# Paired blocks from unit 8, loads held until a transpose is through, a new load order in the lead-in, and V of units 1 to 7 scaled by GpSimd

## The chip, the cores and the metric

The kernel runs on one core of a Trainium2 chip. The metric is device microseconds of that core, median over runs. Before the change it was 311.35 us (three runs, 311.02 to 311.6).

## The reference, cut to what matters

```python
q, k, v: (8 batches, 8 heads, 576 positions, 64)      # float32
scores = q @ k.T / 8;  D[i, j] = gamma_h ** (i - j) if i >= j else 0
attn   = (scores * D) @ v                              # retention, no softmax
x      = attn as (8*576, 512)
h      = x @ w_in;  out = (h * sigmoid(1.702 * h)) @ w_out   # 512 -> 2048 -> 512
```

The kernel cuts the 4608 rows into 36 *units* of 128 rows and keeps a running state k^T v per batch. Four units make a *chunk* of 512 rows for the MLP; `up` is one group of four 512-column matmuls with `w_in`, `down` one group of four with `w_out`. Decay factors go into V (`vfac`) and into the eviction of the result (`gq`).

Of the kernel before, what the change touches and what calls it, by code (L numbers as in the profile page):

```python
# [6 lines left out]
AF = mybir.ActivationFunctionType  # L7
# [6 lines left out]
P = 128  # L14
HP = H // 2
# [6 lines left out]
def gamma(h):  # L22
    return 1.0 - 2.0 ** (-5.0 - h)
# [117 lines left out]
def bass_retnet_parallel__then__act_gelu_quick_kernel(  # L141
# [13 lines left out]
    with es:  # L155
# [11 lines left out]
        iota_k = sb("iota_k", [P, 4], FP32)  # L167
        iota_t = sb("iota_t", [P, 1], FP32)
        scr = sb("scr", [P, 1], FP32)
# [40 lines left out]

        def load_v(u, eng="pool"):
            sl = u % NVN
            rows = unit_rows(u)

            def f(e):
                return [
                    e.dma_start(  # L217
                        vn[sl][p0 : p0 + n, :, :],
                        v[b, :, s0 : s0 + n, :].rearrange("h p d -> p h d"),
                    )  # L220
                    for p0, n, b, s0 in rows
                ]
            op(eng, f, writes=[f"vn{sl}"], dma=f"d_vn{sl}_{eng}", ndma=len(rows))

# [44 lines left out]

        def setup_last():  # L270
            for hp in range(HP):
                op("act", lambda e, hp=hp: e.activation(
                    gq[:, 4, hp, :].rearrange("p (t i) -> p t i", i=64),
                    iota_c[:, None, 512:576].to_broadcast([P, 2, 64]),
                    AF.Exp, bias=lnsc.ap(), scale=lng[:, hp : hp + 1]),
                   reads=["iota_c", "lnsc", f"lng{hp}_0", f"lng{hp}_1"], writes=[f"gq{hp}_4"])
            op("dve", lambda e: e.tensor_scalar_add(iota_t[0:64], iota_k[0:64, 0:1], 512.0),
               reads=["iota_k"], writes=["iota_t0"])
            op("dve", lambda e: e.tensor_scalar_add(iota_t[64:128], iota_k[64:128, 0:1], 448.0),
               reads=["iota_k"], writes=["iota_t1"])  # L280
            for h in range(H):
                op("act", lambda e, h=h: e.activation(
                    vfac[:, 4, h : h + 1], iota_t.ap(), AF.Exp, scale=-math.log(gamma(h))),
                   reads=["iota_t0", "iota_t1"], writes=[f"vfact{h}"])

# [4 lines left out]
        def setup_tail():  # L290
            op("dve", lambda e: e.tensor_single_scalar(maskc.ap(), dmat.ap(), 0.0, ALU.is_ge),
               reads=["dmat"], writes=["maskc"])
            op("dve", lambda e: e.memset(maskc[0:64, 64:128], 0.0), reads=["maskc"], writes=["maskc"])
            for j in range(4):
                op("dve", lambda e, j=j: e.memset(kv[1][j].ap(), 0.0), writes=[f"kv1_{j}"])

        VF = [f"vfac{h}" for h in range(H)]
        VFT = [f"vfact{h}" for h in range(H)]

        def scale_v(u):  # L300
            sl, _, ty = u % NVN, *unit_info(u)[1:]
            op("dve", lambda e: e.tensor_tensor(  # L302
                vp[u % NVP].ap(), vn[sl].ap(),
                vfac[:, ty, :, None].to_broadcast([P, H, DH]), ALU.mult),
               reads=[f"vn{sl}"] + (VF if ty < 4 else VFT), writes=[f"vp{u % NVP}"])
# [248 lines left out]
        def head_mid(u):  # L554
            scale_v(u)
            head_s(u)
# [4 lines left out]

        def fetch(m, after=()):
            for u in (2 * m, 2 * m + 1):
                if u < NU:
                    load_kq(u, after)
                    load_v(u)

# [9 lines left out]

        def block(m, done=False):

            a, b = 2 * m, 2 * m + 1  # L580
            nxt = 2 * m + 2 < NU
            if not done:
                inter(a)
                inter(b)
            if nxt:
                scores(a + 2)
                scores(b + 2)
                scores_out(a + 2, 0)
            if not done:
                values(a)  # L590
                values(b)
                values_out(a)
                values_out(b)
            if nxt:
                scores_out(a + 2, 1)
                scores_out(b + 2, 0)
                scores_out(b + 2, 1)
            fetch(m + 4)
            ready_t(m + 3)
            ready_v(m + 2)  # L600

# [18 lines left out]
        setup_gq(1, 4)  # L620
        setup_last()
        for u in range(1, 4):
            load_kq(u)
            load_v(u)
        for i in range(4):
            load_win(i)
        for u in range(4, 8):
            load_kq(u)
            load_v(u)
        for i in range(4):  # L630
            load_wout(i)
        for u in (8, 9):
            load_kq(u)
            load_v(u)

# [14 lines left out]
        scale_v(0)  # L650
        scale_v(1)
        transpose_half(1, 0, "S2", "act")
        warm(4)
        transpose_half(1, 1, "H0", "act")
        head_k(0, "act")
        head_v(0)
        head_s(1)
        scale_v(2)
        transpose_half(2, 0, "S2", "act")
        warm(2)  # L660
        transpose_half(2, 1, "H0", "act")
        head_k(1, "act")
        head_s(2)
        scale_v(3)
        head_v(1)
        transpose_half(3, 0, "S2", "act")
        transpose_half(3, 1, "H0", "act")
        head_k(2, "act")
        setup_gelu()
        head_s(3)  # L670
        head_v(2)
        warm(3)
        head_v(3)
        head_k(3, "act")
        setup_tail()
        for u in (10, 11):
            load_kq(u)
            load_v(u)
        warm(2)
        play(16, lambda f: up(0, f), {  # L680
# [6 lines left out]
        })  # L687
        fetch(6)
        head_mid(6)
        head_in(7, "dve")  # L690
        warm(1)
        play(8, lambda i: up_half(1, i, 0), {
            1: [lambda: head_out(6)],
# [3 lines left out]
        play(8, lambda i: up_half(1, i, 1), {  # L697
            2: [lambda: head_in(8, "dve")],
            4: [lambda: head_mid(8)],
            6: [lambda: head_out(8)],  # L700
            7: [lambda: head_in(9, "dve")],
        })
        ready_t(6)
        fetch(7, [f"qkT{13 % NQT}q"])
        play(16, lambda i: down(0, i, ("H0", "H1")), {
            1: [lambda: head_mid(9)],
            3: [lambda: head_in(10, "dve"), lambda: head_out(9)],
            5: [lambda: head_mid(10)],
            7: [lambda: head_in(11, "dve"), lambda: head_out(10), lambda: ready_t(7), lambda: fetch(8, [f"qkT{15 % NQT}q"])],
            9: [lambda: head_mid(11), lambda: ready_v(6)],  # L710
            11: [lambda: head_out(11)],
        })
        late = None
        for m in range(5, NU // 2 + 1):
            if m < NU // 2:
                block(m, m == 5)
            if late is not None:
                up(*late)
            c, h = divmod(m - 1, 2)
            iu = idn = 0  # L720
            for x in "UUDDUDUDUDUDDDUU" if m == 5 else "DDUDUDUDUDUDDUUU":
                if x == "D":
                    down(c - 1, 8 * h + idn, YB)
                    idn += 1
# [70 lines left out]
```

## The kernel before: the parts that the change and the argument touch

One helper records every operation and derives the semaphore waits from the tiles it reads and writes. Each engine executes its own list in order, also GpSimd and SyncE, which issue the DMAs.

```python
NLD, NVN, NQT, NVP = 12, 10, 10, 6          # buffers of k/q, V, transposed k/q, scaled V

def load_kq(u, after=()): ...                # two loads on the GpSimd queue, float32 -> bf16
def load_v(u, eng="pool"): ...               # one load on the GpSimd queue
def scale_v(u): op("dve", ... vp[u % NVP] = vn * vfac ...)          # VectorE
def transpose_pe(u, bank, eng): ...          # 8 TensorE transposes and one eviction
def transpose_dma(u):                        # the same by a DMA transpose, on the SP queue
    op("sp", lambda e: e.dma_start_transpose(qkT[u % NQT].ap(), ...), ...)

def scores(u, sb0=None): ...     # 8 matmuls on half the array's rows, banks S0,S1 or S2,S3
def scores_out(u, hh, ...): ...  # VectorE: mask product PSUM -> pm
def values(u, ...): ...          # 8 matmuls on half the array's columns, bank O0 or O1
def inter(u, ...): ...           # q times the running state, whole array
def down(c, i, ybanks): ...      # 4 matmuls; every 4th: ScalarE evicts to osb (4 buffers),
                                 # SP issues the output DMA

def fetch(m, after=()):
    for u in (2 * m, 2 * m + 1):
        if u < NU:
            load_kq(u, after)
            load_v(u)
def ready_t(m): ...              # transpose_dma of units 2m, 2m+1
def ready_v(m): ...              # scale_v of units 2m, 2m+1

def block(m, done=False):        # the steady part: two units at a time
    a, b = 2 * m, 2 * m + 1
    ...
    inter(a); inter(b)
    scores(a + 2); scores(b + 2); scores_out(a + 2, 0)
    values(a); values(b); values_out(a); values_out(b)
    scores_out(a + 2, 1); scores_out(b + 2, 0); scores_out(b + 2, 1)
    fetch(m + 4); ready_t(m + 3); ready_v(m + 2)
# [cut] units 0 to 11 are done one at a time, between the up and down groups of chunks 0 and 1,
# with transpose_pe; pairs and DMA transposes start with unit 12
```

## Time and profile before

| | before |
|---|---|
| time, median | 311.35 us |
| span of the profiled execution | 309.3 us |
| first `up` group starts | 19.28 us |
| TensorE waits after that, summed from matmul starts | 0.71 us |
| median DMA transpose, issue to landing | 7.5 us |

In the profile PE is TensorE's matmuls, PEld its weight loads, DVE VectorE, ACT ScalarE, POOL GpSimd, SP the SyncE queue. Lines of the kernel before and, one higher, of the changed kernel: L454/L455 `up`, L471/L472 `up` in half chunks, L485/L486 `down`, L414/L415 scores, L433/L434 values, L395/L396 and L402/L403 `inter`, L347/L348 the state products, L423/L424 the mask product, L302/L303 `scale_v`, L203 loads of k and q, L217 loads of V, L493/L494 ScalarE's eviction of the output; L311/L312 are whole-unit TensorE transposes, L325/L326 those by halves, L338/L339 the DMA transpose.

The page's first part (engine, busy time, share of the span, instructions) and its chain of waits by engine:

```profile
PE 302.5 (98%) x2185; PEld 157.7 (51%) x2185; DVE 135.8 (44%) x273; ACT 123.2 (40%) x225; POOL 105.9 (34%) x132
...
PE 92%; POOL 3%; DMA 2%; DVE 2%; issue 0%; POOLq 0%
```

The chain is TensorE nearly throughout. The busy share alone would not prove that. The Trainium skill ("Trainium Kernel Development and Optimization", section Performance Expectations) warns that matmul busy time is a bad measure because matmuls are pipelined. This trace agrees: a 512-column matmul is 379 ns long in it, and the next starts after 216. What can be used is the distance between matmul starts: 216 ns after a 512-column matmul, 109 after 256 columns, 56 after 128.

The timeline of TensorE (start, length, line, operation, shapes, count, idle time before and what ended it) shows the two other things that the argument needs:

```profile
31.84 1.03 PE L454 MATMUL psH<-xT,w_in_sb 128*128 128x512 bf16 x4
32.80 0.24 PE L433 MATMUL psO<-pm_0,vp 128*64 128x128 bf16 x1
32.80 0.24 PE L433 MATMUL psO<-pm_1,vp 128*64 128x128 bf16 x1
...
36.30 0.24 PE L433 MATMUL psO<-pm_0,vp 128*64 128x128 bf16 x1
36.81 0.24 PE L433 MATMUL psO<-pm_1,vp 128*64 128x128 bf16 x1 [0.26 <-DVE pm_1 L423]
...
40.55 0.24 PE L433 MATMUL psO<-pm_0,vp 128*64 128x128 bf16 x1
40.80 0.24 PE L433 MATMUL psO<-pm_1,vp 128*64 128x128 bf16 x1
```

From 31.84 to 32.80 is 0.96 us for four matmuls whose pitch makes 0.86: the change from the whole array to half-array matmuls costs about 95 ns. Near 36 and 40 us, the two halves of the value products start 0.51 and 0.25 us apart, where they otherwise start 4 ns apart, as at 32.80: they wait for VectorE.

### The profile page before, as it was taken

How to read it: one execution, taken by the hardware profiler on the slowest of the kernel's cores; microseconds unless marked ns; L12 is line 12 of the kernel's file. 1: busy time of each engine (PE TensorE's matmuls, PEld its weight loads, DVE VectorE, ACT ScalarE, POOL GpSimd, SP SyncE). 2: the span in 40 equal slices, each digit the busy share in tenths (PEclk: the TensorE clock that was granted, in tenths of full speed). 3: DMA queues.
4: the chain of work that ended last, by engine and by line, in shares of the span. 5: the costliest groups of instructions: out<-in, count | busy, mean ns of one | idle time of the engine just before them, and what ended most of it. 6: DMA issues, size and time to landing. Idle time of an engine off the chain costs nothing.

```text
span 309.3 us, 5184 instructions
## 1 busy us (share of the span) xinstructions
PE 302.5 (98%) x2185; PEld 157.7 (51%) x2185; DVE 135.8 (44%) x273; ACT 123.2 (40%) x225; POOL 105.9 (34%) x132
## 2 busy tenths in 40 slices
PE   7799999999999999999999999999999999999996
PEld 3444588655454545454545454545545454544444
DVE  6772984597445442546262715271717250100000
ACT  9766345301433333333333333434243434344411
POOL 9999933015699965354326000000000000000000
PEclk9999999999999999999999999999999999999999
DMA  9999999999999999999999999232310101010122
GB/s 156 182 207 188 189 205 180 176 191 156 179 154 226 207 165 188 134 189 130 156 164 192 159 84 178 78 60 72 66 55 16 42 28 34 36 56 31 48 52 86
DMA packets 113895, 39.40 MB, mean 127 GB/s; under 512 B 102800, under 2 KB 107152, under 8 KB 113872
## 3 DMA queue, kind: packets, MB, share of 16 engines
q0 software_dynamic: 80016, 22.55, 73.1%
q1 hardware_dynamic: 33856, 16.52, 30.4%
q8 instruction: 17, 0.28, 0.4%
q14 instruction: 6, 0.05, 0.1%
HBM read 36.70 MB, written 9.44 MB: 149 GB/s over the span
## 4 chain that ended last, share of the span: by engine, by line
PE 92%; POOL 3%; DMA 2%; DVE 2%; issue 0%; POOLq 0%
PE psH L454 36%; PE psS L485 33%; PE psH L471 5%; PE psH L485 5%; PE psO L433 3%; PE psS L414 3%; PE psS L347 2%; DMA vn<-in_v_dram 2%; POOL kq L203 2%; PE psO L395 1%; PE psO L485 1%; PE psS L311 1%; POOL vn L217 1%; PE psS L511 1%; PE psO L511 1%; DVE vp L302 0%
## 5 line engine op out<-in xcount | busy, mean ns | idle before, releaser
L454 PE MATMUL psH<-xT,w_in_sb 128*128 128x512 bf16 x512 | 127.3, 379 | 0.0
L459 ACT ACTIVATE gT<-psH 128x512 bf16<-128x512 f32 x128 | 76.5, 597 | 116.0 <-PE psH L454 116.0
L485 PE MATMUL psS<-w_out_sb,gT 128*128 128x512 bf16 x480 | 117.3, 379 | 0.0
L454 PEld LDWEIGHTS psH<-xT,w_in_sb 128*128 128x128 bf16 x512 | 47.8, 98 | 58.7 <-ACT gT L459 3.2
L485 PEld LDWEIGHTS psS<-w_out_sb,gT 128*128 128x128 bf16 x480 | 46.1, 98 | 51.7
L203 POOL DMA_DIRECT2D kq<-in_k_dram x39 | 36.4, 947 | 52.4 <-DMA qkT<-kq 22.6
L217 POOL DMA_DIRECT2D vn<-in_v_dram x39 | 36.8, 960 | 6.3 <-DVE pm_1 L423 4.3
L423 DVE TENSOR_TENSOR pm_0<-psS,mask 128x512 bf16<-128x512 f32 x32 | 22.0, 688 | 37.5 <-PE psS L414 37.4
L203 POOL DMA_DIRECT2D kq<-in_q_dram x39 | 36.0, 940 | 4.6 <-issue 4.4
L493 ACT ACTIVATE osb<-psS 128x512 f32<-128x512 f32 x30 | 17.9, 597 | 30.3 <-PE psS L485 30.3
L443 DVE TENSOR_TENSOR xT<-psO,gq 128x512 bf16<-128x512 f32 x36 | 23.5, 683 | 11.4 <-PE psO L433 11.4
L302 DVE TENSOR_TENSOR vp<-vn,vfac 128x512 bf16<-128x512 f32 x36 | 23.7, 686 | 2.3 <-DMA vn<-in_v_dram 2.2
L423 DVE TENSOR_TENSOR pm_1<-psS,mask 128x512 bf16<-128x512 f32 x32 | 21.8, 681 | 0.0
L377 DVE TENSOR_TENSOR kvf<-psS,kvf 64x256 f32<-64x256 f32 x24 | 10.1, 421 | 26.3 <-PE psS L347 26.1
L517 DVE COPY osb<-psS 128x256 f32<-128x256 f32 x1 | 0.4, 425 | 41.4 <-PE psS L511 41.4
L471 PE MATMUL psH<-xT,w_in_sb 128*128 128x256 bf16 x128 | 15.2, 273 | 0.0
L485 PE MATMUL psH<-w_out_sb,gT 128*128 128x512 bf16 x64 | 15.0, 380 | 0.0
L476 ACT ACTIVATE gT<-psH 128x512 bf16<-128x512 f32 x16 | 9.6, 598 | 11.5 <-PE psH L471 11.5
L414 PE MATMUL psS<-qkT 64*128 64x128 bf16 x288 | 12.2, 218 | 1.3 <-ACT qkT L330 1.3
L433 PE MATMUL psO<-pm_1,vp 128*64 128x128 bf16 x144 | 12.5, 223 | 0.6 <-DVE pm_1 L423 0.6
L433 PE MATMUL psO<-pm_0,vp 128*64 128x128 bf16 x144 | 13.1, 224 | 0.0
L375 DVE COPY kvf<-psS 64x256 f32<-64x256 f32 x12 | 5.1, 421 | 18.2 <-PE psS L347 18.1
(84 smaller groups left out, 187.1 us busy)
## 6 DMA issues: line engine op xcount, KB each, us to landing
vn<-in_v_dram POOLq DMA_DIRECT2D x31, 256.0 KB, 17.7
out_dram<-osb SPq DMA_DIRECT2D x31, 256.0 KB, 2.5
kq<-in_k_dram POOLq DMA_DIRECT2D x31, 128.0 KB, 16.5
kq<-in_q_dram POOLq DMA_DIRECT2D x31, 128.0 KB, 17.5
w_in_sb<-in_moe_w_in_dram POOLq DMA_DIRECT2D x4, 512.0 KB, 11.4
w_out_sb<-in_moe_w_out_dram POOLq DMA_DIRECT2D x4, 512.0 KB, 19.6
out_dram<-osb SPq DMA_DIRECT2D x10, 128.0 KB, 2.4
vn<-in_v_dram POOLq DMA_DIRECT2D x8, 128.0 KB, 21.3
```

The lines of the kernel that those rows point to most:

```text
L203: e.dma_start(kq[sl][p0 : p0 + n, i, :].rearrange("p (h d) -> p h d", d=DH), src[b, :, s0 : s0 + n, :].rearrange("h p d -> p h d"),)
L217: e.dma_start(vn[sl][p0 : p0 + n, :, :], v[b, :, s0 : s0 + n, :].rearrange("h p d -> p h d"),)
L302: op("dve", lambda e: e.tensor_tensor(vp[u % NVP].ap(), vn[sl].ap(), vfac[:, ty, :, None].to_broadcast([P, H, DH]), ALU.mult), reads=[f"vn ...
L414: op("pe", lambda e, hp=hp, hh=hh, bank=bank: e.matmul(by_pair(bank)[:, hp, :], qt[64 * hh : 64 * hh + 64, hp, :], qt[64 * hh : 64 * hh + ...
L423: op("dve", lambda e: e.tensor_tensor(pm[u % 4][hh].ap(), by_pair(bank), m[:, None, :].to_broadcast([P, HP, P]), ALU.mult), reads=[bank, " ...
L433: op("pe", lambda e, hp=hp, hh=hh: e.matmul(ob[64 * hh : 64 * hh + 64, hp, :], vp[u % NVP][:, 2 * hp + hh, :], pm[u % 4][hh][:, hp, :], st ...
L443: op("dve", lambda e: e.tensor_tensor(xT[ch % 3][:, :, 128 * j : 128 * j + 128], by_pair(bank), gq[:, ty, :, :], ALU.mult), reads=[bank] + ...
L454: op("pe", lambda e, a=a: e.matmul(hb, w_in_sb[:, a, P * f : P * f + P], xT[c % 3][:, a, :], start=(a == 0), stop=(a == HP - 1)), reads=[f ...
L459: op("act", lambda e: e.activation(gT[c % 2][:, f, :], hb, AF.Gelu_apprx_sigmoid), reads=[bank], writes=[f"gT{c % 2}_{f}"])
L471: op("pe", lambda e, a=a, f=f, j=j: e.matmul(hb[:, j, :], w_in_sb[:, a, P * f : P * f + P], xT[c % 3][:, a, n], start=(a == 0), stop=(a == ...
L485: op("pe", lambda e, f=f: e.matmul(y, gT[c % 2][:, f, P * r : P * r + P], w_out_sb[:, f, :], start=(f == 0), stop=(f == NF - 1)), reads=[f ...
L493: op("act", lambda e: e.activation(osb[o].ap(), y, AF.Copy), reads=[bank], writes=[f"osb{o}"])
```

## The change

Its intent: do units 8 to 11 in pairs like the later ones (fewer array changes), transpose 10 and 11 by DMA (less TensorE work), keep the loads of later units off the DMA engines until the transpose of the first unit of a pair is through (only the loads of V carry the wait; k and q stand behind them in GpSimd's list), get k and q of units 2 and 3 before V of the unit ahead of them in the lead-in, and take V scaling of units 1 to 7 from VectorE to GpSimd. Some setup moves as well. Cut to its core:

```diff
-        def scale_v(u):
+        def scale_v(u, eng="dve"):
-        def fetch(m, after=()):
+        def fetch(m, held=None):
+            after = () if held is None else [f"qkT{held % NQT}q"]
             for u in (2 * m, 2 * m + 1):
                 if u < NU:
-                    load_kq(u, after)
-                    load_v(u)
+                    load_v(u, "pool", after)
+            for u in (2 * m, 2 * m + 1):
+                if u < NU:
+                    load_kq(u)
@@ block
-            fetch(m + 4)
-            ready_t(m + 3)
-            ready_v(m + 2)
+            if m > 4:
+                ready_t(m + 3)
+                fetch(m + 4, 2 * m + 6)
+                ready_v(m + 2)
@@ lead-in [TensorE's order there changes too; cut]
-        for u in range(1, 4):
-            load_kq(u)
-            load_v(u)
-        for i in range(4):
-            load_win(i)
+        load_kq(1); load_kq(2); load_v(1); load_kq(3); load_v(2); load_v(3)
+        load_win(0); load_win(1)
+        scale_v(1, "pool"); load_win(2)
+        scale_v(2, "pool"); load_win(3)
+        scale_v(3, "pool")
@@ after the lead-in
+        scale_v(4, "pool"); scale_v(5, "pool")
+        load_kq(8); load_kq(9)
+        scale_v(6, "pool"); scale_v(7, "pool")
+        for u in range(8, 12):
+            load_v(u)
+        load_kq(10); load_kq(11)
@@ units 8 to 11, around the up groups of chunk 1 and the down groups of chunk 0
+        ready_t(5); fetch(6, 10); ready_t(6)
         play(16, lambda i: down(0, i, ("H0", "H1")), {
-            1: [head_mid(9)], 3: [head_in(10, "dve"), head_out(9)], ...   # one unit at a time
+            1: [state(9)],
+            5: [ready_v(5)],
+            6: [block(4)],
+            9: [state(10), fetch(7, 12)],
+            11: [state(11)],
+            12: [ready_v(6)],
+            14: [ready_t(7), fetch(8, 14)],
         })
@@ chunk 1's down groups
-            for x in "UUDDUDUDUDUDDDUU" if m == 5 else ...
+            for x in "DDDDBDDUDDUUUUUUU" if m == 5 else ...      # B: block(5)
-                    down(c - 1, 8 * h + idn, YB)
+                    down(c - 1, 8 * h + idn, ("S2", "S0") if m == 5 else YB)
```

More of the change, by code (lines that the diff above doesn't have):

```diff
@@ L167, in bass_retnet_parallel__then__act_gelu_quick_kernel @@
         iota_k = sb("iota_k", [P, 4], FP32)
-        iota_t = sb("iota_t", [P, 1], FP32)
+        g64 = sb("g64", [P, HP], FP32)
         scr = sb("scr", [P, 1], FP32)
@@ L209, in load_kq, with load_v @@
                 op("pool", f, reads=after, writes=[f"kq{sl}_{i}"], dma=f"d_kq{sl}_{i}", ndma=len(rows))
-        def load_v(u, eng="pool"):
+        def load_v(u, eng="pool", after=()):
             sl = u % NVN
@@ L222, in f @@
                 ]
-            op(eng, f, writes=[f"vn{sl}"], dma=f"d_vn{sl}_{eng}", ndma=len(rows))
+            op(eng, f, reads=after, writes=[f"vn{sl}"], dma=f"d_vn{sl}_{eng}", ndma=len(rows))
         def load_win(i):
@@ L268, in setup_gq, with setup_g64 @@
                    writes=[f"gq{hp}_{c}" for c in range(c0, c1)])
-        def setup_last():
-            for hp in range(HP):
-                op("act", lambda e, hp=hp: e.activation(
-                    gq[:, 4, hp, :].rearrange("p (t i) -> p t i", i=64),
-                    iota_c[:, None, 512:576].to_broadcast([P, 2, 64]),
-                    AF.Exp, bias=lnsc.ap(), scale=lng[:, hp : hp + 1]),
-                   reads=["iota_c", "lnsc", f"lng{hp}_0", f"lng{hp}_1"], writes=[f"gq{hp}_4"])
-            op("dve", lambda e: e.tensor_scalar_add(iota_t[0:64], iota_k[0:64, 0:1], 512.0),
-               reads=["iota_k"], writes=["iota_t0"])
-            op("dve", lambda e: e.tensor_scalar_add(iota_t[64:128], iota_k[64:128, 0:1], 448.0),
-               reads=["iota_k"], writes=["iota_t1"])
-            for h in range(H):
-                op("act", lambda e, h=h: e.activation(
-                    vfac[:, 4, h : h + 1], iota_t.ap(), AF.Exp, scale=-math.log(gamma(h))),
-                   reads=["iota_t0", "iota_t1"], writes=[f"vfact{h}"])
+        def setup_g64():
+            op("act", lambda e: e.activation(g64.ap(), lng.ap(), AF.Exp, scale=64.0),
+               reads=[f"lng{hp}_{hh}" for hp in range(HP) for hh in range(2)], writes=["g64"])
         def setup_gelu():
@@ L295, in setup_tail @@
                 op("dve", lambda e, j=j: e.memset(kv[1][j].ap(), 0.0), writes=[f"kv1_{j}"])
+            op("dve", lambda e: e.tensor_tensor(
+                gq[:, 4, :, :].rearrange("p a (t i) -> p a t i", i=64),
+                gq[:, 3, :, None, 64:128].to_broadcast([P, HP, 2, 64]),
+                g64[:, :, None, None].to_broadcast([P, HP, 2, 64]), ALU.mult),
+               reads=["g64"] + [f"gq{hp}_3" for hp in range(HP)],
+               writes=[f"gq{hp}_4" for hp in range(HP)])
+            for h in range(H):
+                for hh in range(2):
+                    op("dve", lambda e, h=h, hh=hh: e.tensor_single_scalar(
+                        vfac[64 * hh : 64 * hh + 64, 4, h : h + 1],
+                        vfac[64 * hh : 64 * hh + 64, 3, h : h + 1],
+                        gamma(h) ** (64.0 * hh - 128.0), ALU.mult),
+                       reads=[f"vfac{h}"], writes=[f"vfact{h}_{hh}"])
         VF = [f"vfac{h}" for h in range(H)]
-        VFT = [f"vfact{h}" for h in range(H)]
-        def scale_v(u):
+        VFT = [f"vfact{h}_{hh}" for h in range(H) for hh in range(2)]
+        def scale_v(u, eng="dve"):
             sl, _, ty = u % NVN, *unit_info(u)[1:]
-            op("dve", lambda e: e.tensor_tensor(
+            op(eng, lambda e: e.tensor_tensor(
                 vp[u % NVP].ap(), vn[sl].ap(),
@@ L554, in head_mid @@
         def head_mid(u):
-            scale_v(u)
             head_s(u)
@@ L576, in ready_v, with scores_of, block @@
                     scale_v(u)
-        def block(m, done=False):
+        def scores_of(m):
+            for u in (2 * m, 2 * m + 1):
+                scores(u)
+            for u in (2 * m, 2 * m + 1):
+                scores_out(u, 0)
+                scores_out(u, 1)
+        def block(m):
             a, b = 2 * m, 2 * m + 1
             nxt = 2 * m + 2 < NU
-            if not done:
-                inter(a)
-                inter(b)
+            inter(a)
+            inter(b)
             if nxt:
@@ L588, in block @@
                 scores_out(a + 2, 0)
-            if not done:
-                values(a)
-                values(b)
-                values_out(a)
-                values_out(b)
+            values(a)
+            values(b)
+            values_out(a)
+            values_out(b)
             if nxt:
@@ L620, in bass_retnet_parallel__then__act_gelu_quick_kernel @@
         setup_gq(1, 4)
-        setup_last()
-        for u in range(1, 4):
-            load_kq(u)
-            load_v(u)
-        for i in range(4):
-            load_win(i)
+        setup_g64()
+        load_kq(1)
+        load_kq(2)
+        load_v(1)
+        load_kq(3)
+        load_v(2)
+        load_v(3)
+        load_win(0)
+        load_win(1)
+        scale_v(1, "pool")
+        load_win(2)
+        scale_v(2, "pool")
+        load_win(3)
+        scale_v(3, "pool")
         for u in range(4, 8):
@@ L631, in bass_retnet_parallel__then__act_gelu_quick_kernel @@
             load_wout(i)
-        for u in (8, 9):
-            load_kq(u)
-            load_v(u)
         def play(n, step, events):
@@ L650, in bass_retnet_parallel__then__act_gelu_quick_kernel @@
         scale_v(0)
-        scale_v(1)
         transpose_half(1, 0, "S2", "act")
@@ L654, in bass_retnet_parallel__then__act_gelu_quick_kernel @@
         transpose_half(1, 1, "H0", "act")
+        head_v(0)
+        transpose_half(2, 0, "S2", "act")
+        head_s(1)
+        transpose_half(2, 1, "H0", "act")
         head_k(0, "act")
-        head_v(0)
-        head_s(1)
-        scale_v(2)
-        transpose_half(2, 0, "S2", "act")
-        warm(2)
-        transpose_half(2, 1, "H0", "act")
-        head_k(1, "act")
-        head_s(2)
-        scale_v(3)
-        head_v(1)
-        transpose_half(3, 0, "S2", "act")
-        transpose_half(3, 1, "H0", "act")
+        warm(1)
+        head_s(2)
+        transpose_half(3, 0, "S2", "act")
+        inter(1)
+        values(1)
+        values_out(1)
+        transpose_half(3, 1, "H0", "act")
+        head_k(1, "act")
+        warm(1)
+        head_s(3)
+        warm(2)
         head_k(2, "act")
+        head_v(2)
         setup_gelu()
-        head_s(3)
-        head_v(2)
-        warm(3)
-        head_v(3)
+        inter(3)
+        values(3)
+        values_out(3)
         head_k(3, "act")
         setup_tail()
-        for u in (10, 11):
-            load_kq(u)
+        scale_v(4, "pool")
+        scale_v(5, "pool")
+        load_kq(8)
+        load_kq(9)
+        scale_v(6, "pool")
+        scale_v(7, "pool")
+        for u in range(8, 12):
             load_v(u)
+        load_kq(10)
+        load_kq(11)
         warm(2)
@@ L687, in bass_retnet_parallel__then__act_gelu_quick_kernel @@
         })
-        fetch(6)
         head_mid(6)
@@ L691, in bass_retnet_parallel__then__act_gelu_quick_kernel @@
         warm(1)
+        ready_t(5)
+        fetch(6, 10)
+        ready_t(6)
         play(8, lambda i: up_half(1, i, 0), {
@@ L697, in bass_retnet_parallel__then__act_gelu_quick_kernel @@
         play(8, lambda i: up_half(1, i, 1), {
-            2: [lambda: head_in(8, "dve")],
-            4: [lambda: head_mid(8)],
-            6: [lambda: head_out(8)],
-            7: [lambda: head_in(9, "dve")],
-        })
-        ready_t(6)
-        fetch(7, [f"qkT{13 % NQT}q"])
+            2: [lambda: head_in(8, "dve", "S2")],
+            4: [lambda: head_in(9, "dve", "S0")],
+            6: [lambda: ready_v(4), lambda: scores_of(4)],
+        })
         play(16, lambda i: down(0, i, ("H0", "H1")), {
-            1: [lambda: head_mid(9)],
-            3: [lambda: head_in(10, "dve"), lambda: head_out(9)],
-            5: [lambda: head_mid(10)],
-            7: [lambda: head_in(11, "dve"), lambda: head_out(10), lambda: ready_t(7), lambda: fetch(8, [f"qkT{15 % NQT}q"])],
-            9: [lambda: head_mid(11), lambda: ready_v(6)],
-            11: [lambda: head_out(11)],
+            1: [lambda: state(9)],
+            5: [lambda: ready_v(5)],
+            6: [lambda: block(4)],
+            9: [lambda: state(10), lambda: fetch(7, 12)],
+            11: [lambda: state(11)],
+            12: [lambda: ready_v(6)],
+            14: [lambda: ready_t(7), lambda: fetch(8, 14)],
         })
@@ L714, in bass_retnet_parallel__then__act_gelu_quick_kernel @@
         for m in range(5, NU // 2 + 1):
-            if m < NU // 2:
-                block(m, m == 5)
+            if 5 < m < NU // 2:
+                block(m)
             if late is not None:
@@ L720, in bass_retnet_parallel__then__act_gelu_quick_kernel @@
             iu = idn = 0
-            for x in "UUDDUDUDUDUDDDUU" if m == 5 else "DDUDUDUDUDUDDUUU":
+            for x in "DDDDBDDUDDUUUUUUU" if m == 5 else "DDUDUDUDUDUDDUUU":
+                if x == "B":
+                    block(m)
+                    continue
                 if x == "D":
-                    down(c - 1, 8 * h + idn, YB)
+                    down(c - 1, 8 * h + idn, ("S2", "S0") if m == 5 else YB)
                     idn += 1
```

## The prediction

> **What bounds the kernel now.** TensorE: 98% busy on the page, 92% of the chain of waits. From the start times of its matmuls in the timeline: a 512-column matmul takes 216 ns to the next, a 256-column one 109, a 128-column one 56. Each change between full-array matmuls and the half-array ones of scores and values adds about 95 ns (an `up` group of four takes 0.97 us before such a group, else 0.86). Summed in program order, the work from the first `up` (19.28 us) to the end is 286.5 us by my estimate; the trace takes 287.4. So after 19.28 us only 0.9 us is stall: 0.45 and 0.19 us at 36.3 and 40.6 us, where values wait for VectorE's second mask product, and crumbs. The lead-in is bounded by loads (V landing, then mask products).
>
> **What the change removes.** (1) Units 10 and 11 are transposed by DMA: 16 TensorE transposes of 56 ns, 0.9 us. (2) Units 8 to 11 become pairs: 10 array changes fewer after the first `up`, 0.95 us. The same sum for the new order is 284.7 us, 1.85 less, all on the critical path. (3) VectorE loses seven V scalings of 0.69 us, so the two mask-product stalls (0.6 us) should go.
>
> **What it adds.** GpSimd scales V of 1 to 7. The Trainium skill ("GPSIMD Engine Reference", Elementwise side-by-side cycle accounting) has 4497 ns for 2048 fp32 columns; a quarter is 1.1 us (estimate; nothing in this trace shows it). They stand in the queue that issues loads (0.88 us each), so later loads are issued up to 5 us later; but loads land 10 to 20 us after issue, so landings hardly move. Sixteen small setup operations fall where VectorE is idle.
>
> **Lead-in.** V of 3 lands as before (15.5 us), is scaled by 17.5, then values and eviction: `up` at 18.8 us instead of 19.3. But q of unit 4, transposed after ten `up` groups, lands at 27.94 us now and is used at 28.14; the bytes ahead of it are the same, so TensorE will wait there and all but 0.1 us of the gain is lost.
>
> **New wait.** Units 10 and 11 need loads, then DMA transposes. Their k and q land about 58.2 and 60.0 us (estimate from present landings); a transpose now takes 3.1 us with little traffic, 4.5 with much. Their scores are wanted at about 62; I expect 62.5 to 63.5: a stall of 0.8 us (0 to 2).
>
> **Holding loads** until a transpose is through shortens transposes (median 7.5 us now) in the steady part, where TensorE doesn't wait: worth nothing there. A block takes 15.7 us, a gated round of transpose and six loads about 13, so it should not starve.
>
> **Sum.** 311.35 - 1.85 - 0.6 - 0.1 + 0.8 = 309.6; the new wait may be smaller, since this is tuned. I say 309.4 us, 308.2 to 310.8 in 8 of 10. Faster by over 2%: 0.02; within: 0.965; slower: 0.015.
>
> **What would show it.** Timeline: `up` starting near 18.8, a stall near 27.5 charged to the q load; GpSimd scaling near 1.1 us; no stall at 36 and 40; scores waiting for the transposed tile near 62; from 75 us on, no waits and 1 to 1.9 us ahead of before. Groups: 48 instead of 64 whole-unit TensorE transposes. DMA issues: transposes well under 7.5 us.
>
> **What would make it wrong.** GpSimd scaling far slower than 1.1 us; a faster load stream, giving the lead-in 0.5 us more; transposes of 10 and 11 later than thought; gated loads starving a block.

## The result, and the profile after

The changed kernel takes 309.78 us (median of six runs, 309.47 to 310.51) against 311.6 us of the kernel before in the same rounds; ratio 0.9945, 95% interval 0.9927 to 0.9963. The interval lies below 1: the gain of about 1.7 us is real. A ratio here is always the mean time of one kernel's fast runs over the mean of the other's fast runs of the same rounds, so it is not quite the ratio of the medians quoted beside it.

The profiled execution of after spans 308.4 us. Busy times and chain:

```profile
PE 297.2 (96%) x2133; PEld 156.7 (51%) x2168; DVE 134.8 (44%) x279; ACT 121.3 (39%) x214; POOL 113.0 (37%) x139
...
PE 73%; POOL 13%; DMA 11%; issue 2%; SPq 0%; ACT 0%; DVE 0%; POOLq 0%; ACTq 0%
```

The trace holds 2168 weight loads but only 2133 matmuls: 35 records are missing, and idle times of 0.16 to 0.22 us charged to "issue" in it are such holes. The 96% come from these holes too: a0_after below, the same kernel with all 2168 records, shows 98%, as before. The chain has changed its nature. Part of it, cut to 56 to 82 us (start, length, what):

```profile
44.88 13.78 DMA kq<-in_q_dram
...
58.74 3.30 DMA qkT<-kq
...
63.05 1.77 POOL vn L217 x2
64.83 2.59 POOL kq L203 x3
67.41 5.89 DMA kq<-in_q_dram
...
73.38 1.23 SPq L339
74.61 0.05 issue
74.67 2.37 DMA out_dram<-osb
...
77.12 0.61 ACT osb L494
77.72 0.05 issue
77.77 0.40 PE psS L415 x8
```

Read it upwards from 77.77 us. Unit 13's scores wait for ScalarE to evict bank S2. ScalarE waits for an output buffer. That buffer's output DMA was issued only at 74.67 us, because the SP queue stood in order behind the transpose of unit 13 (73.38), which waited for q of unit 13 (issued 67.41). That load was held, with V of 12 and 13, until the transpose of unit 10 (58.74 to 62.04), which waited for q of unit 10. So in this execution a chain of loads sets the time up to 77 us, not TensorE. TensorE's timeline shows two waits:

```profile
62.17 0.40 PE L403 MATMUL psO<-qkT,kv 128*128 128x64 bf16 x8
62.50 0.40 PE L415 MATMUL psS<-qkT 64*128 64x128 bf16 x8
63.39 0.40 PE L415 MATMUL psS<-qkT 64*128 64x128 bf16 x8 [0.49 <-DMA qkT<-kq]
...
76.64 0.40 PE L415 MATMUL psS<-qkT 64*128 64x128 bf16 x8
77.77 0.40 PE L415 MATMUL psS<-qkT 64*128 64x128 bf16 x8 [0.73 <-ACT osb L494]
```

Beyond its normal pitch, the scores of unit 11 come 0.65 us late and those of unit 13 0.89 us late. The waits for VectorE near 36 and 40 us are gone: the first two lines below are the same value products. GpSimd's scaling (group by line) and the transposes (DMA issues, last figure us to landing; before it was 7.5):

```profile
36.40 0.41 PE L434 MATMUL psO<-pm,vp 128*64 128x128 bf16 x8
40.15 0.41 PE L434 MATMUL psO<-pm,vp 128*64 128x128 bf16 x8
...
L303 POOL TENSOR_TENSOR vp<-vn,vfac 128x512 bf16<-128x512 f32 x7 | 7.5, 1125 | 2.1 <-DMA vn<-in_v_dram 2.1
...
qkT<-kq SPq DMA_TRANSPOSE x26, 3.2
```

From the scores of block 6 (89.87 us before, 88.94 after) to those of block 16, both traces take 158.01 us. Nothing was gained or lost in the steady part; everything happens before 90 us.

### The profile page after: what moved, and what is told of

Same layout as the page of the kernel before. It is cut to its first block, busy times and chain, and to the rows that moved or that the text cites. A ratio compares the mean times of both kernels' runs of the same rounds, so it can differ in the third digit from the quotient of the medians.

```text
span 308.4 us, 5131 instructions
## 1 busy us (share of the span) xinstructions
PE 297.2 (96%) x2133; PEld 156.7 (51%) x2168; DVE 134.8 (44%) x279; ACT 121.3 (39%) x214; POOL 113.0 (37%) x139
## 4 chain that ended last, share of the span: by engine, by line
PE 73%; POOL 13%; DMA 11%; issue 2%; SPq 0%; ACT 0%; DVE 0%; POOLq 0%; ACTq 0%
PE psS L486 32%; PE psH L455 31%; POOL kq L203 6%; DMA kq<-in_q_dram 6%; POOL vn L217 3%; PE psO L434 2%; DMA vn<-in_v_dram 2%; PE psS L415 2%; POOL vp L303 2%; PE psS L348 2%; PE psO L396 1%; PE psO L486 1%; DMA qkT<-kq 1%; POOL w_out_sb L232 1%; DMA out_dram<-osb 1%
## 5 line engine op out<-in xcount | busy, mean ns | idle before, releaser
L455 PE MATMUL psH<-xT,w_in_sb 128*128 128x512 bf16 x489 | 123.5, 379 | 2.4 <-issue 1.7
L486 PE MATMUL psS<-w_out_sb,gT 128*128 128x512 bf16 x472 | 115.9, 379 | 0.5 <-issue 0.2
L455 PEld LDWEIGHTS psH<-xT,w_in_sb 128*128 128x128 bf16 x512 | 47.8, 98 | 58.4 <-ACT gT L460 3.5
L217 POOL DMA_DIRECT2D vn<-in_v_dram x39 | 33.7, 882 | 93.3 <-DMA qkT<-kq 77.9
L424 DVE TENSOR_TENSOR pm<-psS,mask 128x512 bf16<-128x512 f32 x64 | 41.3, 683 | 41.1 <-PE psS L415 41.0
L203 POOL DMA_DIRECT2D kq<-in_k_dram x39 | 34.8, 899 | 0.0
L303 DVE TENSOR_TENSOR vp<-vn,vfac 128x512 bf16<-128x512 f32 x29 | 18.8, 684 | 1.4 <-DMA vn<-in_v_dram 1.3
L381 DVE CAST kv<-kvf 64x256 bf16<-64x256 f32 x36 | 13.3, 369 | 1.2
L472 PEld LDWEIGHTS psH<-xT,w_in_sb 128*128 128x128 bf16 x128 | 12.0, 98 | 1.8 <-issue 0.2
L348 PEld LDWEIGHTS psS<-vp,kq 128*128 128x128 bf16 x128 | 9.2, 98 | 7.0 <-ACT kv L361 0.7
L348 PE MATMUL psS<-vp,kq 128*128 128x128 bf16 x128 | 12.4, 219 | 0.2 <-POOL vp L303 0.2
```

The costliest lines, as they stand in the source:

```text
L203: e.dma_start(kq[sl][p0 : p0 + n, i, :].rearrange("p (h d) -> p h d", d=DH), src[b, :, s0 : s0 + n, :].rearrange("h p d -> p h d"),)
L217: e.dma_start(vn[sl][p0 : p0 + n, :, :], v[b, :, s0 : s0 + n, :].rearrange("h p d -> p h d"),)
L303: op(eng, lambda e: e.tensor_tensor(vp[u % NVP].ap(), vn[sl].ap(), vfac[:, ty, :, None].to_broadcast([P, H, DH]), ALU.mult), reads=[f"vn{s ...
L348: op("pe", lambda e, hp=hp: e.matmul(kb[:, hp, :], kq[sl][:, 0, P * hp : P * hp + P], vp[u % NVP][:, 2 * hp : 2 * hp + 2, :], start=(first ...
L424: op("dve", lambda e: e.tensor_tensor(pm[u % 4][hh].ap(), by_pair(bank), m[:, None, :].to_broadcast([P, HP, P]), ALU.mult), reads=[bank, " ...
L455: op("pe", lambda e, a=a: e.matmul(hb, w_in_sb[:, a, P * f : P * f + P], xT[c % 3][:, a, :], start=(a == 0), stop=(a == HP - 1)), reads=[f ...
```

## The experiments

Theory A, from the prediction: TensorE binds, so each saving or wait on it counts fully. Theory B, its rival: up to the landing of unit 11's transpose the load stream binds, so what TensorE saves before that is waited away there. Theory B was formed after the first runs; for e1 to e7 it is an explanation afterwards, and c1 to c3 are its tests. All kernels gave correct results. All are edits of the changed kernel, timed against the kernel before.

| run | change to the changed kernel | median us | ratio to before (95%) |
|---|---|---|---|
| a0_after | none | 309.61 | 0.9945 (0.9932 to 0.9958) |
| e1_bank | another output bank | 309.76 | 0.9941 (0.9930 to 0.9953) |
| e2_late | first pair 0.86 us later | 309.86 | 0.9952 (0.9936 to 0.9969) |
| e3_dve | V scaled by VectorE | 309.69 | 0.9939 (0.9927 to 0.9950) |
| e4_kvorder | old order k, q, V | 310.05 | 0.9968 (0.9950 to 0.9985) |
| e5_petr | TensorE transposes 10 and 11 | 309.56 | 0.9941 (0.9930 to 0.9953) |
| e6_nohold | no load held | 330.24 | 1.0591 (1.0562 to 1.0620) |
| e7_switch | one more array change a block | 311.87 | 1.0012 (1.0000 to 1.0025) |
| e8_headhold | no load held in the steady part | 314.88 | 1.0106 (1.0086 to 1.0126) |
| c1_order | k, q of 10, 11 first, their V held | 309.08 | 0.9913 (0.9900 to 0.9926) |
| c2_orderdve | c1 with V scaled by VectorE | 309.40 | 0.9931 (0.9919 to 0.9944) |
| c3_best | c1, e1, lead-in mended | 308.48 | 0.9904 (0.9888 to 0.9921) |

A difference of 0.001 in ratio is 0.3 us, and most intervals are as wide as 0.4 us to each side, so single steps of 0.3 us can't be told apart here. What follows therefore leans on the traces as well. Marks from one profiled execution each, in us; a wait is the distance between matmul starts less the usual pitch, and waits below 0.1 are written as 0:

| run | first `up` | wait, unit 11 | wait, bank S2 | unit 11's transpose lands | last matmul ends | end less landing |
|---|---|---|---|---|---|---|
| after | 19.38 | 0.65 | 0.89 | 63.34 | 305.75 | 242.41 |
| a0_after | 18.96 | 0.77 | 0.25 | 63.30 | 304.94 | 241.64 |
| e1_bank | 19.12 | 0.93 | 0 | 63.89 | 305.33 | 241.44 |
| e3_dve | 19.46 | 0 | 0 | 63.89 | 305.35 | 241.46 |
| e4_kvorder | 20.34 | 0.1 | 0 | 63.76 | 305.22 | 241.46 |
| c1_order | 19.77 | 0 | 0.30 | 61.21 | 304.76 | 243.55 |
| c3_best | 18.91 | 0 | 0 | 60.75 | 304.08 | 243.33 |

In the first five rows the first `up` differs by 1.38 us, but the end less the landing of unit 11's transpose, with the bank's wait taken off as well, lies between 241.39 and 241.52 us. This is theory B in one column. (In e3_dve and e4_kvorder TensorE came just as the transpose landed; runs whose edit changes the work behind the landing are left out.) In the last two rows the landing no longer binds, and the difference is 2 us larger. What delays the landing is not the issue of the loads: with VectorE scaling in e3_dve, GpSimd issued q of unit 11 at 37.92 us, 8.5 us earlier than in a0_after (46.37), yet it landed at 60.77 against 59.97.

### a0_after: the base

> The changed kernel unaltered, beside the kernel before in the same rounds, as the base for the other runs. Expected ratio 0.994 to 0.995 again (about 1.7 us). Its profile should again show TensorE waiting about 0.6 us for the DMA transpose of unit 11 near 63 us and 0.9 us near 77 us for ScalarE's eviction of the output bank that the scores of unit 13 want.

Measured as expected, except that the bank's wait was 0.25 us and not 0.9. The same kernel thus varies: its first `up` started at 19.38 us in one profile and 18.96 in the other. In nine profiles with this lead-in (these two, e1_bank, e2_late, e5_petr to e8_headhold, c1_order) it started at 18.96 to 19.77 us, 19.34 on average; the one profile of the kernel before has 19.28. A gain in the lead-in is thus not seen.

### e1_bank: is the wait for the bank lost time?

> One bank name changed: the first output rows of the second chunk are accumulated in H0, idle at that time, instead of S2, which the scores of unit 13 want at once. Theory: the 0.9 us wait near 77 us is lost time on the critical path; it vanishes and the run is 0.8 to 0.95 us shorter than a0_after. Rival: everything behind it is bound by the held loads and transposes, or the wait only moves; then within 0.3 us of a0_after.

```diff
-                    down(c - 1, 8 * h + idn, ("S2", "S0") if m == 5 else YB)
+                    down(c - 1, 8 * h + idn, ("H0", "S0") if m == 5 else YB)
```

The wait is gone: both units' scores now run as one group.

```profile
76.52 0.61 PE L396 MATMUL psO<-qkT,kv 128*128 128x128 bf16 x8
77.06 0.62 PE L415 MATMUL psS<-qkT 64*128 64x128 bf16 x16
```

The time hardly moved: ratio 0.9941 against 0.9945. The expected 0.8 to 0.95 us is a miss. In this profile the transpose of unit 11 landed 0.6 us later than in a0_after and its wait was 0.93 us. The bank's wait was 0.25 us in one profile and 0.89 in the other, so its mean may well be a few tenths, which these intervals can't resolve. What stays open is its mean size, not that it exists.

### e2_late: is the wait for unit 11 lost time?

> The first paired block is placed one group of four output matmuls (0.86 us) later, so that the transposed units 10 and 11 have landed when their scores come. Theory: the 0.65 us wait near 63 us goes and the run is 0.5 to 0.7 us shorter than a0_after. Rival: the later block pushes the values and states behind it and the time comes back; then the same as a0_after.

```diff
-            6: [lambda: block(4)],
+            7: [lambda: block(4)],
```

No gain (0.9952). The profile shows why: scores of unit 11 still waited 0.35 us (this execution's transpose landed at 64.08 us), and the state products of units 10 and 11 now collide, a new wait of 0.4 us near 66 to 69 us for VectorE to evict their bank. So the rival was right that the time comes back, in part through the collision and in part because the landing itself varies.

### e3_dve: what is GpSimd's scaling worth?

> V of units 1 to 7 scaled by VectorE again, all else as changed. Theory: the two waits of values for VectorE near 36 and 40 us come back (0.6 us together), the lead-in is within 0.3 us (loads bind it, and GpSimd's 1.04 us is slower than VectorE's 0.69): 0.3 to 0.7 us longer than a0_after. Rival: GpSimd scaling delays load issues and the lead-in so much that VectorE is as good or better: same or shorter than a0_after.

```diff
         def head_mid(u):
+            scale_v(u)
             head_s(u)
@@ lead-in; all scale_v(.., "pool") removed
+        scale_v(1)
         head_s(2)
...
+        scale_v(2)
         head_s(3)
+        scale_v(3)
```

The waits for VectorE came back as expected, here the larger one:

```profile
36.84 0.24 PE L434 MATMUL psO<-pm,vp 128*64 128x128 bf16 x1
37.34 0.41 PE L434 MATMUL psO<-pm,vp 128*64 128x128 bf16 x7 [0.26 <-DVE pm L424]
```

But the time did not grow (0.9939). TensorE arrived later at unit 11's scores and found its transpose landed: both units' scores run as one group, without a wait.

```profile
63.70 0.64 PE L415 MATMUL psS<-qkT 64*128 64x128 bf16 x16
```

The 0.66 us of waits for VectorE had only replaced a wait that came anyway. So in the changed kernel GpSimd's scaling of V brings nothing measurable, and theory A fails.

### e4_kvorder: what is the load order worth?

> Only the order of the loads of units 1 to 3 goes back: k, q, V of each unit in turn. Theory: V of unit 3 and the loads behind it land as before, and they bind the lead-in, so the first up group starts within 0.3 us of the changed kernel and the whole is within 0.3 us. Rival: k and q ahead of V are what shortens the lead-in; then the first up group starts 0.5 us or more later, and the whole is that much longer.

```diff
-        load_kq(1); load_kq(2); load_v(1); load_kq(3); load_v(2); load_v(3)
+        for u in range(1, 4):
+            load_kq(u)
+            load_v(u)
```

```profile
9.87 0.41 PE L434 MATMUL psO<-pm,vp 128*64 128x128 bf16 x8
11.82 0.38 PE L326 MATMUL psS<-ident,kq 128*128 128x128 bf16 x4 [1.53 <-DMA kq<-in_k_dram]
...
20.34 0.82 PE L455 MATMUL psH<-xT,w_in_sb 128*128 128x512 bf16 x3
```

The rival was right about the lead-in. With TensorE's new order there, k of unit 2 is wanted at about 10 us, and with V ahead of it TensorE waits 1.5 us; the first `up` starts at 20.34 us. About the whole it was not shown to be right. The ratio is 0.7 us longer (0.9968 against 0.9945), but the intervals overlap, and three of the six runs had a granted clock of 0.988 to 0.994. The three at full clock average 309.81 us (0.9948), no more than the changed kernel; the others average 310.75. Whether this load order brings the lower clock is open, as none of those three was profiled. In the profile, at full clock, the late start is taken up by the wait for unit 11, which shrank from 0.77 to 0.1 us.

### e5_petr: what do DMA transposes of 10 and 11 bring?

> Units 10 and 11 transposed by TensorE again (pairs kept, the hold of the loads of 12 and 13 dropped with it). 16 transposes of 56 ns are 0.9 us more TensorE work; the 0.65 us wait for the DMA transpose goes. Theory: 0.2 to 0.4 us longer than the changed kernel, so the DMA transposes as placed bring little. Rival: the wait was not lost time, and the whole 0.9 us is seen.

```diff
-        ready_t(5)
-        fetch(6, 10)
+        fetch(6)
         ready_t(6)
@@
             1: [lambda: state(9)],
+            3: [lambda: head_in(10, "dve", "S2")],
+            4: [lambda: head_in(11, "dve", "S0")],
             5: [lambda: ready_v(5)],
```

The run takes the same time as the changed kernel (0.9941; the expected 0.2 to 0.4 us more lies within the intervals), and after the first `up` only 0.29 us of waits in its profile. Sixteen transposes of 56 ns, 0.9 us, buy off the two waits. So the DMA transposes, placed as they are, save 0.9 us of TensorE work and give it back as waiting.

### e6_nohold and e8_headhold: what is holding the loads worth?

> No load is held for a transpose. Theory: V and k, q of 12 and 13 then compete with the transposes of 10 and 11, which land 1 to 3 us later than 62.0 and 63.3 us, and the wait of the scores near 63 us grows by as much, so 1 to 3 us longer than the changed kernel; later stages don't wait. Rival: holding is worth nothing (transposes queue behind nothing that matters): the same as the changed kernel.

```diff
-            after = () if held is None else [f"qkT{held % NQT}q"]
+            after = ()
```

The run takes 18 us more than the kernel before, far beyond what either theory had said. The one profile of this kernel is slow (span 333.5 us, mean clock 0.964), so it is used only to see where the waits are:

```profile
62.32 0.40 PE L403 MATMUL psO<-qkT,kv 128*128 128x64 bf16 x8
75.47 0.61 PE L415 MATMUL psS<-qkT 64*128 64x128 bf16 x8 [12.75 <-DMA qkT<-kq]
81.11 0.61 PE L415 MATMUL psS<-qkT 64*128 64x128 bf16 x8 [5.03 <-DMA qkT<-kq]
```

The transpose of unit 10 was issued at 59.04 us and landed at 75.42; with the hold it is issued at 58.74 and lands at 62.04. The difference is in the loads beside which it runs: without the hold, twelve loads of units 12 to 15 have been issued and not landed when it starts. The Trainium skill ("DMA: Bandwidth & Descriptors", Queues, rings and completion order) says that each DMA engine goes round its queues packet by packet. That fits a transpose slowed five times by loads of another queue, but no run here shows the mechanism. The granted clock falls as well, as the skill describes after an idle window of about 3.4 us ("TensorE: Matmul & The Clock Gate", Part 1). After the wait of 12.75 us had begun it was half of full speed from 66.5 to 87.0 us, so the matmuls behind the waits ran at half speed too; part of the loss is that.

> The holds of loads 12 to 17 stay, those of the steady part (blocks 6 and later) are dropped. e6_nohold dropped all and cost 19 us. Theory of the prediction: holding is worth nothing in the steady part, where transposes have slack of a block and more: within 0.4 us of the changed kernel, transposes twice as long or more. Rival: without holds loads pile up ahead of the transposes there too and a block starves: 2 us or more longer, with a wait of scores for a transposed tile after 110 us.

```diff
                 ready_t(m + 3)
-                fetch(m + 4, 2 * m + 6)
+                fetch(m + 4)
                 ready_v(m + 2)
```

The edit frees the loads from units 18 and 19 (block 5) on. The run takes 5.0 us more than the changed kernel (1.0106 less 0.9945, times 311.5).

```profile
104.87 0.40 PE L415 MATMUL psS<-qkT 64*128 64x128 bf16 x8
107.97 0.40 PE L415 MATMUL psS<-qkT 64*128 64x128 bf16 x8 [2.70 <-DMA qkT<-kq]
...
qkT<-kq SPq DMA_TRANSPOSE x26, 9.7
```

Unit 17's transpose was issued at 97.93 us and landed at 107.83, where its scores were wanted at 105. With the hold it lands at 100.98. The wait is not the whole loss: behind it the clock was half of full speed for 3.4 us (108.3 to 111.7), which costs some 1.7 us (estimate: half of it), and it followed an idle time of only 2.70 us, where the skill speaks of about 3.4; the measurement decides. All six runs show the lower clock (0.989 to 0.995). The kernel before holds only the loads of units 14 to 17 and has slow transposes too (median 7.5 us), yet no such wait: it had issued the transposes of units 16 and 17 at 85.93 and 89.17 us, some ten microseconds earlier. That the hold in the head is what makes them late is likely but not shown alone: in e5_petr, where the first hold is gone and units 10 and 11 need no DMA transpose, unit 16's is issued at 90.40 us, and at 96.48 in after. With transposes this late the hold in the steady part is needed. The rival was right, and the prediction's "worth nothing" is refuted for this kernel.

### e7_switch: what does an array change cost?

> In each paired block the products with the state are moved from ahead of the scores to between scores and values: same work, but one more change between full-array and half-array matmuls in each of 13 blocks. Theory: a change costs about 95 ns, so 1.2 us longer (0.9 to 1.5) than the changed kernel. Rival: changes are hidden by the weight loads and cost nothing in sum: same time.

```diff
-            inter(a)
-            inter(b)
             if nxt:
                 scores(a + 2)
                 scores(b + 2)
                 scores_out(a + 2, 0)
+            inter(a)
+            inter(b)
             values(a)
```

The run takes 2.1 us more than the changed kernel (1.0012 less 0.9945), more than expected. A block had three changes and now has four: scores use half the rows and values half the columns, and going from one to the other costs as much (146 ns from the last score to the first value product in a0_after, 53 between pairs of scores). The steady part gives the clean figure, from the value products of block 6 to those of block 16:

```profile
90.90 0.64 PE L434 MATMUL psO<-pm,vp 128*64 128x128 bf16 x16
...
249.98 0.64 PE L434 MATMUL psO<-pm,vp 128*64 128x128 bf16 x16
```

That is 159.08 us, 1.07 more than the 158.01 of the changed kernel (89.49 to 247.50), for ten more changes: 107 ns each, and 1.4 us over 13 blocks. (Marks at the scores would mislead: the moved products of the first and the last block are not equally many.) The rest is in the head, where the scores are now asked for earlier, before the state products, and wait longer:

```profile
PE psS L415 <- DMA qkT<-kq: 1.1, 2, 0.8
PE psS L415 <- ACT osb L494: 1.0, 1, 1.0
```

(Line of the waiter, what it waited for, us in total, times, longest.) The Trainium skill ("TensorEngine Tiling (Array Packing)", Key Properties) says that a change of tiling mode drains the TensorE, without a figure. This trace agrees that a change costs time and gives a figure: 107 ns in this experiment, about 95 from single starts.

### c1_order: take the load stream out of the way

> Theory B, formed after the first runs: up to about 63 us the changed kernel is bound by the load stream, which ends there in the transpose of unit 11; what TensorE saves before it is waited away at it. Here k and q of 10 and 11 are loaded ahead of V of 10 and 11, which are held until the transpose of 10 is through; the scaling of V10, V11 and the states of 10 and 11 move two groups later. Theory B expects unit 11's q to land near 58 instead of 60 us, its transpose near 61.5 instead of 63.5, no wait of the scores near 63 us, and 0.6 to 1.2 us less than the changed kernel (ratio 0.991 to 0.993). Rival: time is bound elsewhere, or the held V now makes the wait: ratio 0.994 to 0.996.

```diff
-        for u in range(8, 12):
-            load_v(u)
+        load_v(8)
+        load_v(9)
         load_kq(10)
         load_kq(11)
@@
         ready_t(5)
+        for u in (10, 11):
+            load_v(u, "pool", [f"qkT{10 % NQT}q"])
         fetch(6, 10)
@@
-            5: [lambda: ready_v(5)],
-            6: [lambda: block(4)],
-            9: [lambda: state(10), lambda: fetch(7, 12)],
-            11: [lambda: state(11)],
+            6: [lambda: block(4), lambda: ready_v(5)],
+            9: [lambda: fetch(7, 12)],
+            11: [lambda: state(10)],
             12: [lambda: ready_v(6)],
+            13: [lambda: state(11)],
```

q of unit 11 landed at 57.90 us and its transpose at 61.21. The scores of both units run as one group, without a wait:

```profile
62.57 0.40 PE L403 MATMUL psO<-qkT,kv 128*128 128x64 bf16 x8
62.90 0.62 PE L415 MATMUL psS<-qkT 64*128 64x128 bf16 x16
```

The ratio is 0.9913: 1.0 us less than the changed kernel, as theory B said, and the intervals do not overlap. The chain on the page is TensorE's again, where the changed kernel had 73 and 77% in its two profiles:

```profile
PE 92%; DMA 3%; POOL 3%; SPq 0%; issue 0%; ACT 0%; DVE 0%; POOLq 0%; ACTq 0%
```

### c2_orderdve: does GpSimd's scaling count now?

> c1_order with V of units 1 to 7 scaled by VectorE. Scaling on VectorE cost nothing in the changed kernel (e3_dve). Theory B says only because the wait for the transpose of unit 11 took up the 0.6 us of waits for VectorE near 36 and 41 us. With that wait gone they must show: 0.4 to 0.9 us longer than c1_order. Rival: GpSimd scaling is worth nothing at all: the same as c1_order within 0.3 us.

The edit is that of e3_dve on c1_order. It takes 0.56 us longer than c1_order (0.9931 less 0.9913, times 311.5). The same edit cost nothing in the changed kernel. In the profile the waits for VectorE, 0.45 and 0.21 us, are there again:

```profile
35.86 0.24 PE L434 MATMUL psO<-pm,vp 128*64 128x128 bf16 x1
36.36 0.41 PE L434 MATMUL psO<-pm,vp 128*64 128x128 bf16 x7 [0.26 <-DVE pm L424]
...
76.23 0.40 PE L415 MATMUL psS<-qkT 64*128 64x128 bf16 x8
77.02 0.40 PE L415 MATMUL psS<-qkT 64*128 64x128 bf16 x8 [0.39 <-ACT osb L494]
```

The two intervals just overlap, so the size is uncertain; sign and size fit theory B and not its rival. But the profiles do not isolate the waits for VectorE as the cause. The first `up` started 1.08 us earlier here (18.69 us against 19.77), the scores of unit 12 start at the same time (76.23 and 76.24), and the bank's wait behind them is longer (0.55 against 0.30); the last matmul ends 0.24 us later. A c2 with e1_bank's free bank was not run. Nor is either engine shown to be better in the lead-in: with VectorE too the first `up` started at 19.46 us in e3_dve.

### c3_best: a version meant to beat both

> A version meant to beat both: c1_order, the free output bank of e1_bank, V of units 1 to 3 scaled by VectorE and of 4 to 7 by GpSimd, k and q of unit 4 loaded ahead of the last quarter of w_in. In the profiles the first up group followed the landing of V of unit 3 by 2.8 us with VectorE scaling (c2_orderdve) and 3.4 us with GpSimd (c1_order); the bank wait was 0.3 us in c1_order. Theory B: both now count, 0.5 to 0.9 us less than c1_order, ratio to before 0.988 to 0.990. Rival: the landing of the first quarter of w_in binds the first up group, and only the bank's 0.3 us shows: ratio 0.990 to 0.992.

```diff
         load_win(1)
-        scale_v(1, "pool")
         load_win(2)
-        scale_v(2, "pool")
+        load_kq(4)
         load_win(3)
-        scale_v(3, "pool")
-        for u in range(4, 8):
+        load_v(4)
+        for u in range(5, 8):
@@ scale_v(1), scale_v(2), scale_v(3) on VectorE as in e3_dve; c1_order and e1_bank besides
```

308.48 us, ratio 0.9904: 3.0 us less than the kernel before and 1.3 us less than the changed kernel. Over c1_order it is only 0.3 us, within the intervals: theory B's 0.5 to 0.9 us is a miss, and the ratio lies in the rival's range (binding by `w_in`). The profile backs the rival: the first `up` waits for the first quarter of `w_in`.

```profile
18.91 1.46 PE L455 MATMUL psH<-xT,w_in_sb 128*128 128x512 bf16 x6 [0.32 <-DMA w_in_sb<-in_moe_w_in_dram]
```

## Why the prediction was right or wrong, point by point

- **The time: right, in part by luck.** 309.4 us predicted, 309.78 measured, inside 308.2 to 310.8; the last paragraph shows which errors cancelled.
- **TensorE's saving of 1.85 us: right in size, wrong that it all counts.** The groups show 48 instead of 64 whole-unit transposes, and e7_switch confirms the cost of an array change (107 ns, 95 assumed). But the transposes' 0.9 us came back as waits (e5_petr).
- **The 0.6 us of waits for VectorE: gone in the trace, but worth nothing in the time** (e3_dve), until the wait behind them was removed (c2_orderdve, 0.56 us, which fits but is not isolated). The step that failed is adding this term to the sum while the sum also held a wait that follows it.
- **GpSimd at 1.1 us: right**, 1.125 us mean in the profile. The figure in the Trainium skill ("GPSIMD Engine Reference", Elementwise side-by-side cycle accounting), scaled to a quarter, held.
- **The lead-in: wrong in detail.** First `up` at 18.8 us was predicted. Nine profiles of the changed lead-in showed 18.96 to 19.77, 19.34 on average, against 19.28 before: no gain is seen. V of unit 3 landed at 16.02 us in after, not 15.5, and its scaling started at 16.97, because the issue of the last quarter of `w_in` stands between the two scalings in GpSimd's list. The cap that was predicted, q of unit 4, did not bind in after: it landed at 27.85 us and was used after 28.02. In the profiles of e1_bank, c2_orderdve and e3_dve it did make TensorE wait, by 0.13 to 0.36 us. The cap that decides is unit 11's transpose. That landings hardly move was right, though the issue was later than said: q of unit 11 was issued 10 us later (46.62 against 36.40) and landed 1.2 us later (59.96 against 58.77).
- **The new wait for unit 11: right.** 0.8 us (0 to 2) predicted, 0.65 and 0.77 measured. What it means was missed: it turns everything ahead of it into slack.
- **"From 75 us on, no waits": wrong.** The output bank S2 is wanted by unit 13's scores while ScalarE waits for an output buffer whose DMA stands behind a transpose in the SP queue: 0.25 to 0.89 us. The order on the SP queue had not been looked at.
- **Holding loads "worth nothing" in the steady part: half right.** Against the kernel before it gains nothing there (158.01 us for ten blocks in both). But dropping it costs 5.0 us (e8_headhold), because this kernel issues its transposes some 10 us later than the kernel before, and the wait there was followed by 3.4 us at half clock; dropping all holds costs 20 us (e6_nohold). The step that failed is the claim of slack: it was read from the trace of before, whose transposes start earlier.

How the total came out all the same can be added up from the marks. From before to a0_after the first `up` moves from 19.28 to 18.96 us (-0.32), the waits after it grow from 0.71 to 1.24 us (+0.53), and TensorE's time without these waits falls by 1.96: together -1.75, the difference of the ends of the last matmuls (306.69 and 304.94). The prediction had -0.1, -0.6 + 0.8 = +0.2 and -1.85. Its wrong terms were each below half a microsecond and of opposite sign. That they cancelled is luck. It also differs between executions: in after, the first `up` came 0.10 us later than before, and the waits of unit 11 and the bank alone were 1.54.

## What to carry to other kernels

When a change adds a wait on a load, everything ahead of that wait on the same engine stops counting: before adding up the savings, find the last arrival that all of them run into, and compare end time less that arrival across runs. Transposes by DMA that are wanted soon need the loads kept out of their way, and a queue that also carries outputs passes a late transpose on to them. If two parts of a change look worthless one by one, test them again after the binding arrival is moved.

## What the Trainium skill lacked or had wrong

- "DMA: Bandwidth & Descriptors", Rules for kernel authors, says that a transpose next to ordinary DMAs needs nothing. That is about correctness; for time it lacks the cost: a transpose of 128 x 1024 bf16 took 3.2 us median with loads held, 7.5 in the kernel before, 9.7 in e8_headhold, and 16.4 for unit 10 in e6_nohold (slow).
- "TensorEngine Tiling (Array Packing)", Key Properties, has the drain on a change of tiling mode, but no figure: 107 ns for each in e7_switch, about 95 from single starts.
- "GPSIMD Engine Reference" times a two-input operation at 2048 columns only and gives a rate per element beside it; at 512 columns, float32 to bf16 with one broadcast operand, it was 1.125 us here, a quarter of that time, so no large fixed part shows.
